# Cosformer attention with a gated MLP on one Trainium2 core: another written order of operations for chunks 3 to 6, with raw loads that wait for each other

## The chip, the cores and the metric

The kernel runs on one core of a Trainium2 chip. The metric is device time in microseconds (us), from start to end of the program on that core; the profile of one such execution shows what each engine did. The engines are TensorE (PE, with its weight loads PEld), VectorE (DVE), ScalarE (ACT), GpSimd (POOL) and SyncE (SP), which here only issues DMAs.

## What is computed

The inputs are q, k and v of shape 8 x 8 x 576 x 64 (batch, heads, positions, head size), and the MLP's `w_in` (512 x 2048), `w_out` (2048 x 512) and `beta` (2048). All are float32, and so is the output of 4608 x 512.

```python
def phi(x, c, s):
    r = np.maximum(x, 0.0)
    return np.concatenate([r * c, r * s], axis=-1)
kv = np.einsum('bhsf,bhsd->bhfd', phi(k), v)
z = np.sum(phi(k), axis=2)
num = np.einsum('bhsf,bhfd->bhsd', phi(q), kv)
den = np.einsum('bhsf,bhf->bhs', phi(q), z)[..., None] + 1e-06
x = (num / den), heads side by side        # 4608 x 512
h = x @ w_in
g = h * (1.0 / (1.0 + np.exp(-beta * h)))
out = g @ w_out
```

Here c and s are cosine and sine of an angle that grows with the position. The attention is linear: per batch and head a 64 x 65 state is summed over all positions, and the numerators and the denominator are products with it.

## The kernel before

**Tiles and chunks.** The MLP runs over 9 chunks of 512 tokens (c = 0 to 8); the attention runs over 8 batches (b = 0 to 7) of 576 tokens, and is laid into the chunks. Chunks 0 to 2 have orders of their own. Chunks 3 to 6 run through one list of names, `ORDER` (L835), chunks 7 and 8 through `ORDER_END` (L842), which has no attention. In chunk c the attention works at batch b = c + 1, prepares keys and values of batch b + 1 and queries of batch b + 2. The order of the list is the order in which `chunk` (L876) issues, and each engine works through its own part of it in that order. Nothing else schedules: waits between engines follow from the data and the buffers.

**A chunk's h phase** makes h and its silu. Four pairs of columns X, Y, Z and V are made by a fast scheme of seven half-size products each (`h_fast`, L456: X1 to X7, and so on); eight further blocks of 128 columns are plain products of four matmuls (p0 to p7, L419), each followed by a silu on ScalarE (sp0 to sp7). Of a pair, `c1` and `cu` are copies on ScalarE, `c5`, `a2`, `a3` and `a7` a copy and three additions on VectorE (`a7` reads the bank that product 4 goes on to write), and `Sa` and `Sb` the two silus. Each chunk uses sums of halves of x as well (t1 to t4, L850), made near the end of the chunk before. `K` is the state of batch b (72 matmuls, L272), `kt` its copy out of PSUM, and sXY (L397) are sums of silu results on VectorE.

**The o phase** begins at `N0`, the numerators of batch b: 144 small matmuls of 65 columns (L293), with a weight load each, in three thirds into PSUM banks 0, 6 and 4. Then come fourteen products of eight matmuls (`o_fast`, L525): ox1 to ox7 and oy1 to oy7, with their copies (c1o, c5o, cuo, c4x, and the same for y) on ScalarE and additions (o2x, o3x, o7x, and for y) on VectorE. Products x5 and y5 share a PSUM bank, and so do x2 and y2. Beside them stand x0, x1 and x2 (denominators, reciprocals and division, three VectorE operations each, and then a DMA transpose into the layout of the MLP, `x_part`, L767); v0 to v8 on ScalarE and w0 to w8 on VectorE, which scale v of batch b + 1 by sine and cosine (L217, L219); k0 to k3, relus of keys on ScalarE; q0 and q1, relus of queries on VectorE (`q_relu`, L196); and g0 and g1, products of turned queries with a tangent on GpSimd (`q_tan`, L255), of which g0 waits for the last sum s that the list has ahead of it.

**Loads and turns.** `load_raw` (L76) issues a DMA of 1,152 KB on SyncE's queue. There is one raw buffer each for q, k and v. `prep` (L857) issues the next load of a kind when the last name of a set has been taken: for k when k0 to k3 and x0 to x2 have been issued, for v after all of v and w, and for queries, after q0, q1 and x0 to x2, first the query turn (`q_turn_dma`, L251, a DMA transpose of the relued queries) and then the load. SyncE issues in this order, and a wait of one DMA holds back those behind it. Output rows are stored by GpSimd's queue up to chunk 6.

```python
        take = prep(b, [
            ({"k0", "k1", "k2", "k3"} | xs_all, lambda: raw_next("k")),
            ({"q0", "q1"} | xs_all, q_next),
            ({f"{o}{n}" for o in "vw" for n in range(NQ)}, lambda: raw_next("v"))])
```

`H_COLS` and `O_COLS` (L848) say which plain products and o products have their matmuls, except the first, issued in two halves of the columns.

Of the kernel before, what the change touches and what calls it, by code (L numbers as in the profile page):

```python
# [22 lines left out]
def kernel(  # L23
# [14 lines left out]
    nc = tc.nc  # L38
# [15 lines left out]
    one = ctx.enter_context(tc.tile_pool(name="one", bufs=1))  # L54
# [12 lines left out]


    raws = {}

    def raw_tile(b, name):
        if (name, b) not in raws:
            raws[name, b] = raw_pool.tile([P, 4, NQ, D], FP32, name=f"raw_{name}", tag=f"raw_{name}")
        return raws[name, b]

    def load_raw(b, name, j0=0, j1=4):  # L76
        js = slice(j0, j1)
        src = {"q": q, "k": k, "v": v}[name][b]
        nc.sync.dma_start(
            out=raw_tile(b, name)[:, js].rearrange("q j n d -> q j (n d)"),  # L80
            in_=src.rearrange("(j g) (p n) d -> (g p) j (n d)", g=2, n=NQ)[:, js, :])

    win = [const.tile([P, MI, 512], BF16, name=f"win{i}") for i in range(4)]
    wout = const.tile([P, JT, DM], BF16, name="wout")
# [41 lines left out]
    GJ = [(0, 0), (0, 1), (1, 0), (1, 1)]  # L126

    load_raw(0, "q", 0, 2)
    load_raw(0, "q", 2, 4)
    beta16 = const.tile([JT, P], FP32, name="beta16")  # L130
    nc.scalar.dma_start(out=beta16, in_=moe_beta.rearrange("(j p) -> j p", p=P))
    load_raw(0, "v", 0, 2)
    load_raw(0, "k", 0, 2)
    load_raw(0, "v", 2, 4)
# [164 lines left out]
    def x_rden(bank, slot, n0, n1, jps):  # L299

        w, m = len(jps), n1 - n0
        nv = ps[:, bank : bank + 2, slot * E : (slot + w * m) * E].rearrange("q j (i s e) -> q j i s e", s=w, e=E)
        den = small.tile([P, 2, m, w], FP32, name="den", tag=f"den{m}{w}")
        nc.vector.tensor_tensor(  # L304
            den, nv[:, :, :, :, D],
            eps9[:, n0:n1].unsqueeze(1).unsqueeze(3).to_broadcast([P, 2, m, w]), op=ALU.add)
        rden = small.tile([P, 2, m, w], FP32, name="rden", tag=f"rden{m}{w}")
        nc.vector.reciprocal(rden, den)
        return nv, rden, n0, jps
# [100 lines left out]
    def h_group(c, jt):  # L410
        h_mm(c, jt)
        h_act(c, jt)
# [95 lines left out]
    def o_mm(c, tt, jts, cols=1):  # L508
        o_ps = ps[:, (2, 3, 0, 1)[tt] if c == 0 else 2 + tt % 2]
        for jt in jts:  # L510
            w = DM // cols if jt > 0 else DM
            for m0 in range(0, DM, w):
                nc.tensor.matmul(o_ps[:, m0 : m0 + w], lhsT=gs[c, jt // 4][:, jt % 4, tt * P : (tt + 1) * P],  # L513
                                 rhs=wout[:, jt, m0 : m0 + w],
                                 start=(jt == 0), stop=(jt == JT - 1 and m0 == DM - w))
        if jts[-1] < JT - 1:
            return
        o_sb = osb_pool.tile([P, DM], FP32, name="o_sb", tag="o_sb")
        nc.scalar.copy(o_sb, o_ps)
        store(c, tt, o_sb)  # L520

    def o_part(c, tt, part, cols=1):
        o_mm(c, tt, range(4 * part, 4 * part + 4), cols)
# [123 lines left out]
    got = x_rden(2, 0, 0, 7, (0,))  # L647
# [17 lines left out]
    got = x_rden(0, 0, 0, 7, (1,))  # L665
# [125 lines left out]
    def one_unit(slot):  # L791
        if slot == 0:
            num_rest()
            att_q(2)
            v_half(2, 0)
        elif slot == 4:
            k_all(2)
        elif slot == 6:
            v_half(2, 1)
        elif slot == 7:  # L800
            q_tan(2, 0)
            q_tan(2, 1)
        elif slot == 12:
            kv_all(2)
        elif slot == 13:
            w_sums(0, 4)
        elif slot == 14:
            att_q(3)
            w_sums(4, 8)
        elif slot == 18:  # L810
            for t, bank in enumerate((4, 6, 0)):
                num_all(2, t, bank)
            for t, bank in enumerate((4, 6, 0)):
                x_part(2, t, bank)
            load_raw(4, "q")
            q_tan(3, 0)
            q_tan(3, 1)
        elif slot == 28:
            v_half(3, 0)

    for slot in range(32):
        if slot < 16:
            h_group(1, slot)
        else:
            o_part(1, (slot - 16) // 4, slot % 4, 2 if slot > 21 else 1)
        one_unit(slot)

    def k_piece(b, j):
# [4 lines left out]
            load_raw(b + 1, "k")  # L833

    ORDER = (  # L835
        "Y1 p1 c1Y X1 p0 X5 c1X c5X X2 X6 K sp0 cuX Y6 X3 a2X kt a3X cuY sp1 X7 SaX a7X p2 Y5 X4 c5Y sp2 "
        "Y2 Z1 a2Y Y7 Y3 c1Z p3 SbX a3Y a7Y SaY Z6 V1 Y4 s01 s03 cuZ Z5 Z2 sp3 Z7 s02 c5Z c1V a7Z s04 "
        "a2Z p4 SbY Z3 sp4 Z4 V5 V6 V2 SbZ a3Z c5V cuV p5 s11 SaZ a2V V3 a3V sp5 s12 V7 s21 SaV p6 a7V "
        "sp6 p7 s22 s13 V4 sp7 s23 s14 SbV s24 s31 s33 N0 ox1 s32 c1o s34 ox5 c5o x0 x1 ox6 ox3 w0 cuo "
        "v3 oy1 v2 v6 ox2 x2 v4 c1y ox7 oy6 cuy o3x o7x oy5 v1 oy7 ox4 k1 g0 g1 c5y w3 q0 o2x t1 w6 t3 "  # L840
        "w1 w2 o7y t2 oy3 v0 c4x v5 v8 w4 q1 oy2 o2y o3y t4 v7 k2 k3 k0 w5 oy4 c4y w8 w7")
    ORDER_END = (  # L842
        "X1 Y5 Y1 X5 c5X p0 c1X X3 c1Y X6 cuX X2 Y6 sp0 c5Y cuY a2X p1 X7 a3X a7X p2 SaX Y7 X4 sp1 Y3 "
        "sp2 a7Y Z1 Y2 Y4 a3Y p3 c1Z Z6 V1 SbX s03 Z5 SbY a2Y Z2 V5 cuZ c1V p4 c5Z a2Z Z7 SaY Z3 V6 c5V "
        "s01 a3Z sp3 sp4 cuV V2 SaZ a7Z V3 a3V p5 a2V p6 sp5 SaV V7 sp6 Z4 p7 s02 a7V s11 SbZ V4 s12 s14 "
        "sp7 SbV oy1 ox1 s21 s13 s31 c1y ox2 s22 s32 ox5 c1o ox6 cuo c5o o2x s34 s24 s33 s04 oy2 s23 oy6 "
        "ox3 o3x cuy ox7 oy5 c5y t3 oy7 t1 o2y o7y oy3 o7x t2 oy4 c4y t4 ox4 o3y c4x")
    H_COLS, O_COLS = {3: 1, 4: 5, 5: 2, 6: 4}, {3: ("45", "25734"), 5: ("4", "25734")}  # L848

    def x_sum(c, kind):  # L850
        xt, n = xt_tile(c), NB // 2
# [107 lines left out]
    for c in range(2, NTC):  # L959
        b = c + 1  # L960
# [77 lines left out]
```

## Time and profile before

| what | value |
|---|---|
| median of three runs | 287.22 us (287.01 to 287.71) |
| the profiled execution | 287.27 us |
| its span | 285.5 us |
| TensorE busy | 272.7 us (96%) |
| VectorE busy | 219.8 us (77%) |
| ScalarE busy | 177.7 us (62%) |
| GpSimd busy | 71.3 us (25%) |
| DMA moved | 54.00 MB, mean 189 GB/s |

The span runs from the first to the last instruction; the execution's own time has some 1.8 us around it. A matmul's end is modelled in this profile, so TensorE's rate is read from starts: a product of four matmuls of 512 columns takes 0.86 us from its first start to the next product's, and one of eight matmuls of 256 columns 0.87 us. "idle before" names what an engine waited for; "issue" there means that nothing in the profile explains the wait. A line number is one of the kernel before.

### The profile page before, as it was taken

Reading aid. Unit: us, or ns where it says so; the run is one execution under the profiler, and the core shown is the slowest. Engines: PE = TensorE matmul, PEld = TensorE weight load, DVE = VectorE, ACT = ScalarE, POOL = GpSimd, SP = SyncE. Lnnn points to the kernel's source line nnn. Section 1 sums busy time; section 2 is a strip of 40 time slices with the busy share of each in tenths; the row PEclk is TensorE's granted clock in tenths of the full one; section 3 lists DMA queues with packets and bytes.
Section 4 is the critical chain, followed back from the end, with each engine's and each line's share of the span. In section 5 each row is a group of like instructions: output and inputs, shape, how many; then the busy total and the mean of one; then the engine's idle time right before and its main releaser. Section 6 shows DMA issues by size and latency. Waiting matters only on the chain. (4 is left out here: it accounts for less than half of the span.)

```text
span 285.5 us, 8867 instructions
## 1 busy us (share of the span) xinstructions
PE 272.7 (96%) x3685; PEld 197.2 (69%) x3685; DVE 219.8 (77%) x547; ACT 177.7 (62%) x356; POOL 71.3 (25%) x89
## 2 busy tenths in 40 slices
PE   8799999999999999999997999999999999999992
PEld 7354455455765688778884787688878866886781
DVE  5989967759999996899879876898689457656840
ACT  5778755863146576965786367955794269329710
POOL 1444000634490182015600632053300220000000
PEclk9999999999999999999999799999999999999998
DMA  6999999999989959973797339817400540032014
GB/s 248 378 393 386 391 380 314 318 247 386 164 251 373 268 103 249 192 282 79 154 285 299 57 77 213 304 30 95 113 2 11 113 110 1 2 85 65 0 39 110
DMA packets 50584, 54.00 MB, mean 189 GB/s; under 512 B 31200, under 2 KB 31472, under 8 KB 50544
## 3 DMA queue, kind: packets, MB, share of 16 engines
q1 hardware_dynamic: 47584, 45.82, 56.1%
q0 software_dynamic: 2688, 7.34, 10.2%
q8 instruction: 29, 0.48, 0.7%
q10 hardware_dynamic: 272, 0.27, 0.3%
q14 instruction: 11, 0.09, 0.2%
HBM read 36.71 MB, written 9.44 MB: 162 GB/s over the span
## 5 line engine op out<-in xcount | busy, mean ns | idle before, releaser
L417 ACT ACTIVATE g_t<-ps,beta 128x512 bf16<-128x512 f32 x96 | 61.3, 693 | 3.5 <-PE ps L426 3.1
L536 PEld LDWEIGHTS <-S 128*128 128x128 bf16 x497 | 45.3, 99 | 6.8 <-issue 1.7
L506 POOL DMA_DIRECT2D out_dram<-o_sb x56 | 31.8, 574 | 71.2 <-DVE o_sb L586 33.8
L426 PE MATMUL ps<-xt,win 128*128 128x512 bf16 (+1 forms) x228 | 48.4, 345 | 0.0
L378 PE MATMUL ps<-xt,win 128*128 128x512 bf16 (+1 forms) x196 | 42.8, 375 | 0.1
L386 ACT ACTIVATE g_t<-ps,beta 128x512 bf16<-128x512 f32 x48 | 32.6, 689 | 10.5 <-PE ps L378 9.9
L536 PEld LDWEIGHTS <-g_t 128*128 128x128 bf16 x378 | 33.5, 99 | 3.8
L378 PEld LDWEIGHTS <-win 128*128 128x128 bf16 x196 | 18.8, 98 | 21.0 <-issue 0.2
L426 PEld LDWEIGHTS <-win 128*128 128x128 bf16 x228 | 22.3, 98 | 12.8
L222 POOL TENSOR_TENSOR qs<-qt,tanr 128x1152 bf16<-128x1152 bf16 x8 | 19.4, 2444 | 45.0 <-DVE den L304 30.1
L219 DVE TENSOR_SCALAR vb<-raw_v,cos 128x256 bf16<-128x256 f32 x63 | 29.6, 518 | 0.3 <-DMA raw_v<-in_v_dram 0.3
L536 PE MATMUL ps<-T,S 128*128 128x256 bf16 (+1 forms) x245 | 28.3, 268 | 1.4 <-DVE o_sb L587 1.4
L513 PE MATMUL ps<-wout,g_t 128*128 128x512 bf16 (+1 forms) x166 | 29.2, 330 | 0.0
L536 PE MATMUL ps<-wout,g_t 128*128 128x256 bf16 (+1 forms) x238 | 28.6, 271 | 0.0
L536 PE MATMUL ps<-wout,S 128*128 128x256 bf16 (+1 forms) x252 | 28.1, 261 | 0.0
L465 PE MATMUL ps<-w_stage 128*128 128x256 bf16 x144 | 26.9, 273 | 0.0
L465 PEld LDWEIGHTS <-w_stage 128*128 128x128 bf16 x192 | 18.4, 98 | 7.4
L315 DVE TENSOR_TENSOR xs<-ps,rden 128x768 bf16<-128x768 f32 (+4 forms) x26 | 22.8, 883 | 0.8
L513 PEld LDWEIGHTS <-g_t 128*128 128x128 bf16 x166 | 15.8, 98 | 10.3
L397 DVE TENSOR_TENSOR S<-g_t 128x512 bf16<-128x512 bf16 (+1 forms) x58 | 22.1, 408 | 0.7 <-ACT g_t L417 0.4
L217 ACT ACTIVATE vb<-raw_v,sin 128x256 bf16<-128x256 f32 (+1 forms) x50 | 21.7, 498 | 1.0 <-DMA raw_v<-in_v_dram 1.0
L490 DVE COPY p<-ps 128x256 f32<-128x256 f32 x24 | 9.9, 421 | 10.8 <-PE ps L465 9.5
(104 smaller groups left out, 402.2 us busy)
## 6 DMA issues: line engine op xcount, KB each, us to landing
raw_v<-in_v_dram SPq DMA_DIRECT2D x7, 1152.0 KB, 11.2
raw_k<-in_k_dram SPq DMA_DIRECT2D x7, 1152.0 KB, 10.0
raw_q<-in_q_dram SPq DMA_DIRECT2D x7, 1152.0 KB, 7.8
out_dram<-o_sb POOLq DMA_DIRECT2D x56, 128.0 KB, 4.3
w_stage<-in_moe_w_in_dram SPq DMA_DIRECT2D x3, 1024.0 KB, 13.7
w_stage<-in_moe_w_out_dram SPq DMA_DIRECT2D x2, 1024.0 KB, 8.5
w_stage<-in_moe_w_out_dram SPq DMA_DIRECT2D x4, 512.0 KB, 11.9
out_dram<-o_sb SPq DMA_DIRECT2D x13, 128.0 KB, 2.4
```

The lines of the kernel that those rows point to most:

```text
L217: nc.scalar.activation(o, a, AF.Copy, scale=t[:, n : n + 1])
L219: nc.vector.tensor_scalar(o, a, scalar1=t[:, n : n + 1], scalar2=None, op0=ALU.mult)
L315: nc.vector.tensor_tensor(o.rearrange("q j n s d -> q j (n s) d"), nv[:, :, a:z, :, 0:D].rearrange("q j n s d -> q j (n s) d"), rden[:, :, ...
L378: nc.tensor.matmul(ps[:, h_bank(c, jt), blocks.start * 64 : blocks.stop * 64], lhsT=win[jt // 4][:, mi, (jt % 4) * P : (jt % 4 + 1) * P], ...
L386: nc.scalar.activation(gs[c, jt // 4][:, jt % 4], ps[:, h_bank(c, jt)], AF.Silu, scale=beta[:, jt : jt + 1])
L397: return nc.vector.tensor_tensor(o, l, r, op=op)
L417: nc.scalar.activation(gs[c, jt // 4][:, jt % 4], ps[:, bank], AF.Silu, scale=beta[:, jt : jt + 1])
L426: nc.tensor.matmul(ps[:, bank, o * 64 : z * 64], lhsT=win[jt // 4][:, mi, (jt % 4) * P : (jt % 4 + 1) * P], rhs=xt[:, o:z, jp, g * HP : (g ...
L465: nc.tensor.matmul(dst, lhsT=left[:, g], rhs=right[:, :, g * HP : (g + 1) * HP], start=start and g == 0, stop=stop and g == 1, skip_group_ ...
L506: eng.dma_start(out=out_v[bb, n][:, m0:m1], in_=o_sb[hf * HP : (hf + 1) * HP, m0:m1])
L513: nc.tensor.matmul(o_ps[:, m0 : m0 + w], lhsT=gs[c, jt // 4][:, jt % 4, tt * P : (tt + 1) * P], rhs=wout[:, jt, m0 : m0 + w], start=(jt == ...
L536: nc.tensor.matmul(dst[:, m : m + w], lhsT=left(i), rhs=right[:, i, m : m + w], start=start and i == 0, stop=stop and i == order[-1], skip ...
```

## The change

Three things are edited. First, every load of a batch above 4 gets a wait on the load issued before it: SyncE doesn't issue it until that one has landed. Second, chunks 3 to 6 get another order. In it the relus of queries q0 and q1 stand in the h phase, ahead of a7Z and a3Z; since they are then done when x2 comes, the query turn is issued directly behind x2's turn and the load of k. p7 and the silus of pair V stand ahead of sp7, GpSimd's g0 and g1 behind the last sum, and most of v and w behind x1 and x2. Third, other products are issued in halves of columns: in chunk 1 from slot 20 on instead of 22, and as `H_COLS` and `O_COLS` say.

```diff
+    last_load = []
     def load_raw(b, name, j0=0, j1=4):
-        nc.sync.dma_start(
+        got = nc.sync.dma_start(
+        if last_load and b > 4:
+            tc.add_manual_dep(got.ins, last_load[-1].ins.name,
+                              mybir.DependencyInfo(mybir.DependencyClass.Sync, mybir.DependencyReason.DATA),
+                              reason="one batch load at a time")
+        last_load.append(got)
...
-            o_part(1, (slot - 16) // 4, slot % 4, 2 if slot > 21 else 1)
+            o_part(1, (slot - 16) // 4, slot % 4, 2 if slot > 19 else 1)
...
     ORDER = (
-        "Y1 p1 c1Y X1 p0 X5 c1X c5X X2 X6 K sp0 cuX Y6 X3 a2X kt a3X cuY sp1 X7 SaX a7X p2 Y5 X4 c5Y sp2 "
-        "Y2 Z1 a2Y Y7 Y3 c1Z p3 SbX a3Y a7Y SaY Z6 V1 Y4 s01 s03 cuZ Z5 Z2 sp3 Z7 s02 c5Z c1V a7Z s04 "
-        "a2Z p4 SbY Z3 sp4 Z4 V5 V6 V2 SbZ a3Z c5V cuV p5 s11 SaZ a2V V3 a3V sp5 s12 V7 s21 SaV p6 a7V "
-        "sp6 p7 s22 s13 V4 sp7 s23 s14 SbV s24 s31 s33 N0 ox1 s32 c1o s34 ox5 c5o x0 x1 ox6 ox3 w0 cuo "
-        "v3 oy1 v2 v6 ox2 x2 v4 c1y ox7 oy6 cuy o3x o7x oy5 v1 oy7 ox4 k1 g0 g1 c5y w3 q0 o2x t1 w6 t3 "
-        "w1 w2 o7y t2 oy3 v0 c4x v5 v8 w4 q1 oy2 o2y o3y t4 v7 k2 k3 k0 w5 oy4 c4y w8 w7")
+        "Y1 c1Y X5 X1 c5X c1X p0 X6 Y6 cuX X2 cuY X3 a2X a3X sp0 K X7 p1 kt Z1 Y5 a7X c5Y X4 SaX sp1 SbX "
+        "Y7 a7Y s01 p2 Y2 s03 Z5 a2Y c1Z sp2 Y4 Y3 SbY Z6 Z2 a3Y SaY p4 V5 a2Z c5Z cuZ s02 c5V V1 p3 q0 "
+        "sp4 Z7 V3 c1V V2 V6 a7Z Z3 sp3 Z4 cuV q1 p5 a3Z a2V SbZ V7 SaZ s11 s04 a3V a7V p6 sp5 s12 p7 "
+        "sp6 s13 SaV V4 s21 s23 s14 SbV s22 N0 sp7 ox1 s31 ox5 s32 k1 x0 c1o s33 ox6 k0 k2 k3 c5o oy1 "
+        "s24 ox2 s34 g0 g1 v8 w4 v4 x1 c1y o2x ox3 v2 v7 cuo x2 oy6 ox7 oy2 cuy o3x o7x oy5 oy7 ox4 w8 "
+        "o2y v6 c5y t1 t3 oy3 w1 w0 o7y t2 v5 v3 oy4 t4 o3y w7 v1 w6 c4x w5 w3 w2 v0 c4y")
...
-    H_COLS, O_COLS = {3: 1, 4: 5, 5: 2, 6: 4}, {3: ("45", "25734"), 5: ("4", "25734")}
+    H_COLS, O_COLS = {4: 5, 6: 5}, {3: ("4", "25734"), 4: ("4", ""), 5: ("4", "25734")}
```

## The prediction

> **What bounds the kernel now.** I read the page's shares first: TensorE is busy for 96% of the span, so only its gaps, its clock and its own work can move the end.
>
> ```profile
> PE 272.7 (96%) x3685; PEld 197.2 (69%) x3685; DVE 219.8 (77%) x547; ACT 177.7 (62%) x356; POOL 71.3 (25%) x89
> ...
> PEclk9999999999999999999999799999999999999998
> ```
>
> One slice of the clock row shows a 7, near 160 us. Next I cut the timeline by chunk at each chunk's first product (110.10, 139.39, 171.43, 200.72, 229.20 us): chunks 3 to 6 take 29.29, 32.04, 29.29 and 28.48 us. Gaps between starts of matmuls give what is lost in each. In all four, 0.37 us in the middle of the numerators (L293), which wait for the last silu of pair V to free PSUM bank 4. In chunks 3 and 5, 0.83 and 0.85 us ahead of product oy5, which waits for addition o3x:
>
> ```profile
> 129.79 2.54 DVE L219 TENSOR_SCALAR vb<-raw_v,cos 128x256 bf16<-128x256 f32 x1
> ...
> 133.58 0.41 DVE L587 TENSOR_TENSOR o_sb<-ps,u 128x256 f32<-128x256 f32 x1
> ```
>
> ```profile
> 127.45 4.73 POOL L222 TENSOR_TENSOR qs<-qt,tanr 128x1152 bf16<-128x1152 bf16 x2 [15.18 <-DVE den L304]
> ```
>
> ```profile
> 134.04 0.55 PE L536 MATMUL ps<-T,S 128*128 128x256 bf16 x6 [0.67 <-DVE o_sb L587]
> ```
>
> A scaling that elsewhere takes 0.35 us (w3, 134.24) takes 2.54 us here, and ends as GpSimd's second tangent product does; x2 and o3x stand behind it on VectorE.
>
> Chunk 4 loses most, by windows of 1 us (columns: window, then busy us of each engine, clock, DMA share, GB/s):
>
> ```profile
> 155.00:156.00 1.00, 0.45 (x32) 0.33 (x31) 1.00 (x3) 0.00 (x0) 0.00 (x0) 1.00 0.31 111
> 156.00:157.00 1.00, 0.00 (x0) 0.00 (x0) 0.90 (x5) 0.00 (x0) 0.23 (x1) 1.00 0.08 25
> 157.00:158.00 1.00, 0.72 (x19) 0.56 (x20) 0.96 (x3) 0.00 (x0) 1.00 (x1) 0.77 0.00 0
> 158.00:159.00 1.00, 1.00 (x6) 0.69 (x5) 0.96 (x2) 0.00 (x0) 1.00 (x1) 0.50 0.06 16
> ```
>
> TensorE stops for 2.0 us inside the numerators, and the clock is then 0.50 for 3.4 us (16 products at 213 ns instead of 109: 1.66 us). No engine is named as releaser ("issue"). The DMA queues show what it is:
>
> ```profile
> q8 instruction: 29, 0.48, 0.7%
> ```
>
> 29 blocks of 16 KB are TensorE's some 7,370 instructions[...]. The stall falls at instruction 4,526; the block was fetched only at 154.71 to 155.74, while raw loads filled the DMA (share about 1.0 from 145 to 155), and its predecessor was used up in 1.5 us, as it lay wholly in the numerators (288 instructions).
>
> [...]
>
> **The change, part by part.** Chunk c works with batch b = c+1; q0 and q1 are the relus of batch b+2, so they exist in chunks 3 and 4 only.
>
> *New order of the o phase (gain).* I walked it with the trace's spacings: 0.34 us per addition or sum on VectorE, 1.33 per x part, 0.87 per o product, 0.25 from a product's end to its reader. Numerators start at +14.3 us in the chunk. The last four sums end at +19.2, and only then GpSimd starts; w4 is issued ahead of it; x1, o2x, x2 and o3x read PSUM, and such operations ran beside GpSimd at 127.6 to 129.8. So o3x ends at 19.4+1.3+0.3+1.3+0.4 = +22.8, and oy5, now one product later, begins at +23.8. That stall (0.83, 0.85) goes, with 1 us to spare. Silu SbV moves ahead of sp7; the chain sp6, SaV, SbV still ends at +15.3 against +15.2 needed: 0.2 of the 0.37 stays. o3y no longer comes after oy4: 0.14 saved behind chunk 6. A chunk without waits is 28.48-0.37-0.14 = 27.97 us; with 0.2 and 0.1 for split products, 28.25.
>
> *Columns.* 7 halves more in chunk 1, 3 fewer in chunk 3's p0, 7 moved from chunk 3 to 4, 6 fewer, 3 more: a pair of halves costs 2 to 5 ns more than the whole, under 0.05 us in sum. They move block boundaries: counted in the built order, the numerators of chunks 3 to 6 start 64 after one, 1 after, 78 after and 5 ahead before the change, and 72 after, 5 ahead, 74 after and 3 ahead now. Chunk 4 still has a whole block inside, as chunk 6 has without a stall, where the DMA is idle.
>
> *Relus of queries in the h phase (loss).* The wait is not new, its place is. q0 now stands on VectorE ahead of a7Z, and Z4 on TensorE needs a7Z. Unhindered, q0 would start at +9.5 us and Z4 at +11.1. The h phase otherwise has room: VectorE's 16 additions and copies, kv, 11 sums and two relus are 16x0.34+0.6+11x0.34+2x0.67 = 11.1 us before the numerators at 14.3. What decides is when the raw queries land. For chunk 3 these are batch 6, loaded in chunk 2, which isn't changed:
>
> ```profile
> 105.70 0.92 SPq L79 DMA_DIRECT2D raw_k<-in_k_dram  x1
> 106.79 8.14 SPq L252 DMA_TRANSPOSE qt<-qb  x1
> 115.06 0.50 SPq L79 DMA_DIRECT2D raw_q<-in_q_dram  x1
> ```
>
> ```profile
> raw_q<-in_q_dram SPq DMA_DIRECT2D x1, 1152.0 KB, 10.3
> raw_v<-in_v_dram SPq DMA_DIRECT2D x1, 1152.0 KB, 12.6
> ...
> qt<-qb SPq DMA_TRANSPOSE x1, 14.5
> ```
>
> The turn lands at 121.3, the queries at 115.06+10.3 = 125.4. Before, q0 ran at 134.50. In the trace's packets the load starts at 119.5, when the turn's end, and a load moves in 3 to 3.9 us. Without v's load behind it (now one at a time) it should land at about 124.0 (loads alone land 0.9 us after their last packet: 83.5, 100.7). X5, which moves up to +0.22, waits 0.25 us for the sum of x that chunk 2 ends at 110.51. So Z4, due at 110.1+0.25+11.1 = 121.45, comes at 124.0+0.1+0.67+0.43+0.05 = 125.25: 3.8 us idle (3.0 to 4.1). Such a gap must halve the clock: a gap of 2.0 cost 1.66, so I take 1.6 (0.8 to 2.5). Chunk 3: 28.25+0.25+5.4 = 33.9, +4.6 us.
>
> *Query turn behind x2, loads one at a time.* In chunk 3 SyncE issues k's load at +24.7 (x2's turn, +23.4, takes 1.25), 3.6 us before chunk 4, then the turn; the queries' load (batch 7) waits for k's landing, then runs behind the turn's packets. Unhindered that is k 3, turn 3.2 (140.1 to 143.3), the eight output stores between (1 MB, 4 to 5), q 3.2: landing at +10.5 to +13 of chunk 4. The same sequence took 17.8 us from k's issue at 105.70, which would be +14.2. Before +9.8 nothing waits. I take +12.3: Z4 comes 12.3+1.25-11.1 = 2.5 us late (0 to 4.4), with 1.0 for a clock that drops in part of the cases. v's load then issues at about +12.5 and lands before its readers at +19 (delayed by the same wait). Behind the wait, the block for chunk 4's numerators is asked for before v's packets run: the 2.0 us of fetch and 1.66 of clock go; up to 1.5 if not. Chunk 4: 28.25+3.5 = 31.75, -0.3. In chunk 5 v's load lands about +12, before use. GpSimd's tangents wait for nothing new, its stores go out about 1 us earlier.
>
> *Sum:* +4.6-0.3-1.0 (chunk 5) -0.3 (chunk 6) = +3.0. Chunks 7 and 8 keep their list. The profiled execution took 287.27 us for a span of 285.5, the median is 287.22: the base is the same, 287.3+3.0 = **290.3 us**.
>
> **Rivals.** *Late in both chunks by the longer chain.* Chunk 4 then takes 28.25+4.4+1.7 and 1.5 for the fetch, +3.8: 287.3+4.6+3.8-1.3 = 294.4. For it: k to q took 17.8 us when stores ran beside. *Late in chunk 3 only.* Batch 7 lands by +10: chunk 4 gives 3.1 to 3.8; total 286.7 to 287.5, no change. For it: the two other turns landed 8.8 and 8.9 us after issue, not 14.5. *Faster: the queries are there.* If both loads land before +9.8, every gain stands: -1.0-3.8-1.0-0.3 = -6.1, 281.2 us. It decides at 119.9 us in chunk 3; against it stands that the turn's packets only end then, for it only an earlier turn. *That it doesn't do what it says:* the built order shows q0 ahead of a7Z with waits for both DMAs, so no.
>
> **How the numbers follow.** Forecast (late in both, spread 288.2 to 292.5) 0.62; longer chain 0.10; chunk 3 only 0.18; faster 0.10. About 0.3% is what a measurement of this kernel can tell from no change (286.4 to 288.1). Faster 0.11, same 0.17, slower 0.72. The range leaves out the fastest case and the top of the longer chain: 286.6 to 293.0; the forecast's own is 288.2 to 292.5.
>
> **What would show it.** In chunk 3 VectorE idle before L200's relu of queries until about 124, released by the raw q load, TensorE idle 3.8 us before a product of pair Z with DVE as releaser, and a clock dip there; the same, shorter, in chunk 4; no 2.5 us scaling beside GpSimd; no gap before oy5; no "issue" gap of 2 us in the numerators. I am wrong if batch 6 lands before 121, or if the relu's wait doesn't reach Z4.

## The result and the profile after

The changed kernel takes 297.11 us (median of 294.95, 296.48, 297.73, 302.11) where the kernel before takes 287.47 beside it: a ratio of 1.031, interval 1.024 to 1.037, so it is slower. The prediction said slower, but 290.3 us and at most 293.0. Ratios here and below leave disturbed executions out, so they need not be the quotient of the medians.

The profiled execution of the changed kernel is the one of 294.95 us, the fastest of the four, with a span of 293.0. First the page: TensorE's share, its clock, and the chain that ended last.

```profile
PE 275.6 (94%) x3686; PEld 198.4 (68%) x3686; DVE 216.5 (74%) x547; ACT 178.6 (61%) x356; POOL 71.1 (24%) x89
...
PEclk9999999999999999979998699999999999999999
...
PE ps L542 25%; DMA raw_q<-in_q_dram 13%; PE ps L432 12%; PE ps L384 10%; PE ps L471 9%; PE ps L519 7%; DMA w_stage<-in_moe_w_in_dram 4%; PE ps L299 3%; DMA raw_k<-in_k_dram 3%; SPq L258 2%; PE ps L278 2%; DMA xt<-xs 1%; DVE win L121 1%; SPq L80 1%; PE ps L240 0%
```

Two things are new. The clock row has two dips, a 7 and a 6, where it had one. And in the chain, a load of raw queries carries 13% of the span: the end now hangs on a DMA, where before it hung on TensorE's own work.

TensorE's timeline at the two places (start, duration, engine, line, operation; in brackets idle time before it and what ended it):

```profile
121.41 0.38 PE L471 MATMUL ps<-xt,w_stage 128*128 128x256 bf16 x2
125.89 0.58 PE L471 MATMUL ps<-w_stage,win 128*128 128x256 bf16 x2 [4.09 <-DVE ps L499]
...
155.32 0.38 PE L471 MATMUL ps<-xt,w_stage 128*128 128x256 bf16 x2
160.83 0.58 PE L471 MATMUL ps<-w_stage,win 128*128 128x256 bf16 x2 [5.12 <-DVE ps L499]
```

Each pair of lines is Z3 and Z4. From start to start 4.37 and 5.40 us pass where 0.11 would: Z4 waits for addition a7Z (L499) on VectorE. VectorE's timeline tells why a7Z is late:

```profile
124.73 0.76 DVE L200 TENSOR_SCALAR qb<-raw_q 128x1152 bf16<-128x1152 f32 x1 [4.58 <-DMA raw_q<-in_q_dram]
...
159.67 0.76 DVE L200 TENSOR_SCALAR qb<-raw_q 128x1152 bf16<-128x1152 f32 x1 [5.62 <-DMA raw_q<-in_q_dram]
160.35 0.43 DVE L499 TENSOR_TENSOR ps<-ps,p 128x256 f32<-128x256 f32 x1
```

The relu q0 stands idle until the raw queries land, and a7Z runs directly behind it. Behind the second gap the clock is what costs (windows of 1 us: length, busy us of PE, PEld, DVE, ACT and POOL, clock, DMA share, GB/s):

```profile
158.00:159.00 1.00, 0.00 (x0) 0.00 (x0) 0.00 (x0) 0.00 (x0) 0.00 (x0) 1.00 0.65 240
159.00:160.00 1.00, 0.00 (x0) 0.00 (x0) 0.33 (x1) 0.00 (x0) 0.00 (x0) 0.82 0.01 5
...
161.00:162.00 1.00, 1.00 (x4) 0.43 (x3) 1.00 (x3) 0.55 (x1) 0.00 (x0) 0.50 0.65 164
...
165.00:166.00 1.00, 1.00 (x4) 0.39 (x3) 1.00 (x4) 0.71 (x2) 0.00 (x0) 0.50 0.00 0
166.00:167.00 1.00, 1.00 (x13) 0.37 (x15) 0.01 (x1) 0.55 (x1) 0.00 (x0) 0.76 0.00 0
```

At 158 to 159 no engine works at all and the DMA still moves data. Then p5, V7, p6 and p7 run at 0.50. The dip lasts 6.83 us, twice the 3.41 of chunk 3.

What the loads did is on SyncE's timeline:

```profile
105.97 0.85 SPq L80 DMA_DIRECT2D raw_k<-in_k_dram  x1
106.93 8.06 SPq L258 DMA_TRANSPOSE qt<-qb  x1
115.25 0.37 SPq L80 DMA_DIRECT2D raw_q<-in_q_dram  x1
...
141.93 0.58 SPq L80 DMA_DIRECT2D raw_k<-in_k_dram  x1
142.61 6.90 SPq L258 DMA_TRANSPOSE qt<-qb  x1
149.57 0.85 SPq L80 DMA_DIRECT2D raw_q<-in_q_dram  x1
159.65 0.37 SPq L80 DMA_DIRECT2D raw_v<-in_v_dram  x1
```

SyncE is busy with issuing the query turn for 8.06 and 6.90 us, and until then it issues nothing else. The queries' load of batch 7 goes out at 149.57 and lands 10.0 us later. For half of these its bytes don't move. The DMA queues from 149.6 to 154.6 us (packets, MB, share of the 16 engines' time):

```profile
q1 hardware_dynamic: 877, 0.22, 57.6%
q0 software_dynamic: 232, 0.61, 53.9%
```

q1 is SyncE's queue, q0 GpSimd's with the output stores. 0.22 MB in 877 packets are 256 bytes each, the packets of the turn; a raw load comes in packets of 2,304 bytes. So the turn's packets move, beside the stores, until 155.5, and the queries' begin at 154.9.

The wait before oy5 is gone, as walked. VectorE's scaling w4, which stood at 129.79 for 2.54 us before, GpSimd's tangents, and oy5 on TensorE:

```profile
135.31 0.35 DVE L225 TENSOR_SCALAR vb<-raw_v,cos 128x256 bf16<-128x256 f32 x1
...
135.64 4.73 POOL L228 TENSOR_TENSOR qs<-qt,tanr 128x1152 bf16<-128x1152 bf16 x2 [23.11 <-DVE S L403]
...
140.02 1.05 PE L542 MATMUL ps<-T,S 128*128 128x256 bf16 x15
```

The scaling is over as GpSimd starts and takes 0.35 us; the last line, oy5, has no idle time before it. Why it took 2.54 us beside GpSimd before isn't shown.

### The profile page after: what moved, and what is told of

Same layout as the page of the kernel before. It is cut to its first block, busy times and chain, and to the rows that moved or that the text cites. A ratio compares the mean times of both kernels' runs of the same rounds, so it can differ in the third digit from the quotient of the medians.

```text
span 293.0 us, 8873 instructions
## 1 busy us (share of the span) xinstructions
PE 275.6 (94%) x3686; PEld 198.4 (68%) x3686; DVE 216.5 (74%) x547; ACT 178.6 (61%) x356; POOL 71.1 (24%) x89
## 4 chain that ended last, share of the span: by engine, by line
PE 69%; DMA 22%; SPq 3%; DVE 2%; issue 1%; ACTq 0%; ACT 0%; DVEq 0%
PE ps L542 25%; DMA raw_q<-in_q_dram 13%; PE ps L432 12%; PE ps L384 10%; PE ps L471 9%; PE ps L519 7%; DMA w_stage<-in_moe_w_in_dram 4%; PE ps L299 3%; DMA raw_k<-in_k_dram 3%; SPq L258 2%; PE ps L278 2%; DMA xt<-xs 1%; DVE win L121 1%; SPq L80 1%; PE ps L240 0%
## 5 line engine op out<-in xcount | busy, mean ns | idle before, releaser
L432 PE MATMUL ps<-xt,win 128*128 128x512 bf16 (+1 forms) x222 | 51.9, 369 | 0.0
L542 PEld LDWEIGHTS <-S 128*128 128x128 bf16 x490 | 44.6, 98 | 4.6
L384 PE MATMUL ps<-xt,win 128*128 128x512 bf16 (+1 forms) x196 | 42.8, 375 | 0.1
L542 PEld LDWEIGHTS <-g_t 128*128 128x128 bf16 x385 | 33.6, 98 | 3.5
L384 PEld LDWEIGHTS <-win 128*128 128x128 bf16 x196 | 18.8, 98 | 21.1 <-issue 0.4
L432 PEld LDWEIGHTS <-win 128*128 128x128 bf16 x222 | 22.7, 102 | 15.2 <-issue 3.1
L519 PE MATMUL ps<-wout,g_t 128*128 128x256 bf16 (+1 forms) x173 | 29.3, 324 | 0.0
L542 PE MATMUL ps<-wout,g_t 128*128 128x256 bf16 (+1 forms) x238 | 27.8, 266 | 0.0
L225 DVE TENSOR_SCALAR vb<-raw_v,cos 128x256 bf16<-128x256 f32 x63 | 23.5, 431 | 0.1
L471 PEld LDWEIGHTS <-win 128*128 128x128 bf16 x144 | 14.1, 98 | 13.6 <-issue 10.0
L519 PEld LDWEIGHTS <-g_t 128*128 128x128 bf16 x173 | 16.5, 98 | 9.6
```

Of the source, the lines that this page charges most:

```text
L225: nc.vector.tensor_scalar(o, a, scalar1=t[:, n : n + 1], scalar2=None, op0=ALU.mult)
L384: nc.tensor.matmul(ps[:, h_bank(c, jt), blocks.start * 64 : blocks.stop * 64], lhsT=win[jt // 4][:, mi, (jt % 4) * P : (jt % 4 + 1) * P], ...
L432: nc.tensor.matmul(ps[:, bank, o * 64 : z * 64], lhsT=win[jt // 4][:, mi, (jt % 4) * P : (jt % 4 + 1) * P], rhs=xt[:, o:z, jp, g * HP : (g ...
L471: nc.tensor.matmul(dst, lhsT=left[:, g], rhs=right[:, :, g * HP : (g + 1) * HP], start=start and g == 0, stop=stop and g == 1, skip_group_ ...
L542: nc.tensor.matmul(dst[:, m : m + w], lhsT=left(i), rhs=right[:, i, m : m + w], start=start and i == 0, stop=stop and i == order[-1], skip ...
```

## Where the time went, chunk by chunk

Each chunk is cut at its first product, as in the prediction. Of two profiled executions of the changed kernel the first is the one shown, the second is the run after_again.

| us | before | predicted | after | after_again |
|---|---|---|---|---|
| chunk 3 | 29.29 | 33.9 | 34.12 | 35.36 |
| chunk 4 | 32.04 | 31.75 | 36.07 | 36.67 |
| chunk 5 | 29.29 | 28.3 | 28.15 | 28.14 |
| chunk 6 | 28.48 | 28.2 | 28.07 | 28.08 |

From before to after this is +4.83, +4.03, -1.14 and -0.41; with chunk 3's start 0.26 later it makes +7.57, and the profiled times differ by 294.95 - 287.27 = 7.68. In this execution only chunk 4 is off the prediction by more than 0.3 us. In that of after_again, 296.97 us and nearer to the median, chunk 3 is off by 1.5 us as well.

## The experiments

Chunk times below come from one profile of each kernel (that of swap_both is of an execution of 290.26 us, over its median); the medians of the kernel before, run beside them, were 286.8 to 287.6 us.

| kernel | relus of queries | loads wait | SyncE's order | median us | ratio (interval) | chunk 3 | chunk 4 |
|---|---|---|---|---|---|---|---|
| after_again | h phase | yes | k, turn, q | 297.48 | 1.035 (1.028 to 1.041) | 35.36 | 36.67 |
| no_chain | h phase | no | k, turn, q | 298.24 | 1.037 (1.032 to 1.043) | 36.09 | 37.83 |
| turn_first | h phase | no | turn, k, q | 294.62 | 1.023 (1.019 to 1.027) | 37.37 | 34.31 |
| swap_both | h phase | yes | turn, q, k | 287.89 | 0.996 (0.992 to 0.999) | 32.26 | 33.28 |
| swap_no_chain | h phase | no | turn, q, k | 282.34 | 0.983 (0.977 to 0.989) | 28.39 | 29.12 |
| swap_shift | h phase | no | turn, q, k | 281.60 | 0.981 (0.977 to 0.986) | 28.44 | 28.59 |
| q_late | h phase, later | yes | k, turn, q | 288.64 | 1.000 (0.997 to 1.004) | 30.74 | 32.04 |
| q_back | o phase | yes | k, turn, q | 286.18 | 0.997 (0.994 to 0.999) | 33.00 | 30.26 |
| order_alone | o phase | no | k, turn, q | 285.80 | 0.994 (0.991 to 0.997) | 28.63 | 32.51 |
| order_shift | o phase | no | k, turn, q | 282.59 | 0.984 (0.979 to 0.989) | 28.44 | 29.60 |
| chain_alone | as before | yes | as before | 290.03 | 1.005 (1.003 to 1.008) | 30.51 | 33.95 |
| fetch_shift | as before | no | as before | 285.27 | 0.992 (0.989 to 0.994) | 29.34 | 29.22 |

The kernel warm, without a ratio, follows below. In every kernel with the new order, warm apart, chunks 5 and 6 take 28.14 and 28.07 us within 0.02.

**The theory**: the relus hold Z4 until the raw queries land, and they land late because of what stands ahead of their load on SyncE. **The rivals**: another part of the change costs the time (order, columns, waiting loads), or the waiting loads make the queries late.

### The relus moved back

```diff
-V1 p3 q0 sp4 ... Z4 cuV q1 p5 ... t1 t3 oy3 ... o3y w7
+V1 p3 sp4 ... Z4 cuV p5 ... t1 t3 q0 oy3 ... o3y q1 w7
```

> The changed kernel with q0 and q1 moved back into the o phase (behind t3 and o3y), all else kept. Theory (the relus of queries, standing ahead of a7Z, hold Z4 until the raw queries land): the gaps of 4.3 us before Z4 in chunk 3 and 5.3 us in chunk 4 vanish, and with them the half clock behind each (1.5 and 2.8 us); the time is 281 to 285 us, the upper end if the instruction block of chunk 4's numerators is again fetched late. Rival (another part of the change, such as the columns or the serial loads, slows the kernel): it stays at 292 us or more.

Both gaps before Z4 went, and the time fell to 286.18 us, not to 281 to 285. A new wait took their place: in chunk 3's o phase TensorE lost 4.6 us, 2.5 of them in one gap and most of the rest by the half clock behind it (from 135.24 eight matmuls take 1.66 us instead of 0.87). The timelines of this kernel, VectorE, ScalarE and TensorE:

```profile
132.96 1.80 DVE L225 TENSOR_SCALAR vb<-raw_v,cos 128x256 bf16<-128x256 f32 x1 [3.31 <-DMA raw_v<-in_v_dram]
...
132.96 0.92 ACT L223 ACTIVATE vb<-raw_v,sin 128x256 bf16<-128x256 f32 x2 [3.07 <-DMA raw_v<-in_v_dram]
133.78 0.35 ACT L588 COPY p<-ps 128x256 f32<-128x256 f32 x1
...
134.17 1.03 PE L542 MATMUL ps<-T,S 128*128 128x256 bf16 x8 [2.37 <-ACT p L588]
```

The scalings v8 (ScalarE) and w4 (VectorE) wait for v of batch 5, whose load stands behind the queries' landing and so issued at 126.16 instead of near 116. Behind v8 stands the copy c1y, and oy6 on TensorE needs its bank. In the changed kernel this wait is not seen, since the gap before Z4 had put everything 4 us later. So the change has a second late load under the first.

### Without the waits between loads

```diff
-        if last_load and b > 4:
+        if False:
```

> The changed kernel without the wait of each load on the load before it; order and columns kept. Theory (in chunk 4 the query load was held by SyncE, which was busy 6.9 us with the query turn, not by the wait on k's load): k of batch 7 landed at 148.7 us and the query load was issued at 149.57, so both gaps before Z4 stay within 1 us of 4.3 and 5.3 us; the late instruction block of chunk 4's numerators may return (0 to 3.7 us); 292 to 299 us. Rival (the serial loads make the queries late): chunk 4's gap drops to 2 us or less and the time to 289 us or less.

> The changed kernel with q0 and q1 back in the o phase and without the wait between loads: only the new order of the rest and the columns are left. Theory (the new order gains by itself; what remained in the run with the relus moved back alone, 4.6 us in chunk 3 and 2.0 in chunk 4 of the o phase, was the wait of w4 and v8 for v, whose load was held behind the query load): v's load issues near 116 us instead of 126, no gap in the o phase of chunks 3 to 6, no gap before Z4; 280 to 284 us, the upper end if chunk 4's instruction block is fetched late again. Rival (the order itself makes those gaps): they stay, 285 us or more.

In no_chain (the changed kernel without the waits) neither side was right on chunk 4. The gap didn't fall, which the rival wanted, but grew from 5.3 us to 8.0, where I had allowed 1 us. Chunk 3's gap grew too, to 5.6 us. The query load of chunk 4 was issued at about the same place (+5.5 us in the chunk, +5.1 with the waits) but landed at +17.8 instead of +15.1 (+15.6 in after_again). v's load, issued right behind it at 152.24, is not seen to slow it: by the packets, v's follow the queries', and v landed 3.0 us after them. What took longer is the turn, whose packets ran beside the stores for 11.0 us, until 160.1, against 8.3 us in the changed kernel; why is open. So the queries landed 2.2 to 2.7 us earlier with the waits, without a reason shown.

order_alone (q_back without the waits) shows what the rest of the change is worth: chunk 3 takes 28.63, so nearly all of q_back's 4.6 us were v's late load. Chunk 4 lost 4.0 us again, to the gap in the numerators that the kernel before has too (2.64 us) and to the half clock behind it (0.53 from 158 to 161 us). Its 285.80 us is over the 280 to 284 expected, and meets the rival's number, though not its gaps in the o phase: the range had room for that gap only on top of 280, and the best kernel below, without it, takes 281.6. The four medians are 285.8 and 286.2 with the relus in the o phase, without and with waits, and 298.2 and 297.5 with them in the h phase: the place of the relus costs 11 to 12 us, the waits at most 1.

### The same waits alone

> The kernel before with only the wait of each batch load on the load before it. Theory (the 2.0 us stop in chunk 4's numerators is an instruction block fetched late behind raw loads that fill the DMA): with loads one at a time the block comes earlier, the stop shrinks or goes and the half clock with it, 283.5 to 286 us. Rival (the wait itself delays loads that somebody needs): 288 us or more, with a new gap released by a raw load. Third: the stop is of another origin, 287.2 us with the same 2.0 us gap.

The kernel before with only the waits took 290.03 us: slower by 0.5%, as the rival said. The gap in chunk 4's numerators did shrink, from 2.0 to 1.0 us without a dip, but v's readers then waited in both chunks (1.2 us more in chunk 3). The theory was right on the fetch and wrong on the time.

### The block of instructions

```diff
-    H_COLS, O_COLS = {3: 1, 4: 5, 5: 2, 6: 4}, ...
+    H_COLS, O_COLS = {3: 8, 4: 5, 5: 2, 6: 4}, ...
```

> The kernel before with 8 instead of 1 of chunk 3's plain products issued in halves: 28 more matmuls ahead, so that the boundaries of TensorE's instruction blocks move, and chunk 4's numerators start 43 instructions before a boundary rather than 1 after one. Theory (late instruction block): the 2.0 us stop in the middle of chunk 4's numerators and the 1.66 us of half clock go or move to another place; 283.5 to 285 us, or about 287 if the stop only moves. Rival (the stop belongs to the numerators' data or banks): the gap stays at the same matmul and the time is 287.2 us.

The edit adds 21 matmuls, not 28, each with its weight load: 42 instructions. Chunk 4 went from 32.04 to 29.22 us and the stop with it: 285.27 us. The next test moves the same boundaries in order_alone:

```diff
-    H_COLS, O_COLS = {4: 5, 6: 5}, ...
+    H_COLS, O_COLS = {3: 7, 4: 5, 6: 5}, ...
```

> The run with the new order of the rest alone (relus of queries back in the o phase, no wait between loads), and 7 of chunk 3's plain products in halves: 42 more instructions on TensorE ahead of chunk 4, whose numerators then start 37 after a block boundary rather than 5 ahead of one. Theory (the 4.0 us that chunk 4 lost there, numerators and half clock, are the late instruction block): they go, chunk 4 takes 28.5 us instead of 32.5, 281 to 282.5 us. Rival (the new order feeds the numerators late): the gap stays, 285 us or more.

Here 1.3 us of it stayed (chunk 4 29.60, not 28.5), and just this settles what it is. TensorE's timeline in chunk 4's numerators of order_shift, and then of swap_no_chain, which lacks the 42 instructions:

```profile
153.94 0.21 PE L299 MATMUL ps<-kv,qs 64*64 64x65 bf16 x2
155.45 0.22 PE L299 MATMUL ps<-kv,qs 64*64 64x65 bf16 x2 [1.30 <-issue]
```

```profile
154.41 0.21 PE L299 MATMUL ps<-kv,qt 64*64 64x65 bf16 x3
155.45 0.21 PE L299 MATMUL ps<-kv,qt 64*64 64x65 bf16 x1 [0.82 <-issue]
```

In the first the gap stands 42 instructions earlier in the program, in another product of the numerators. But counted from the program's start it is the same one: in the records of the kernel before, order_alone, order_shift, swap_no_chain and q_late alike, the gap is ahead of TensorE's instruction 4,531 (the prediction had 4,526; 2.02, 2.64, 1.49, 1.01 and 2.92 us from start to start), and in chain_alone and swap_both ahead of 4,525, where a few records can be missing. It belongs to a count, not to a product, so it is the block. The packets of the instruction queue agree: in all seven the gap ends 1.3 to 1.5 us after those of one block do. That also explains fetch_shift. There the block's packets ended at 154.0 us, in order_shift at 154.2; but TensorE reached the count at 155.75 in the first and waited for nothing, and stood before it from 153.96 in the second. What decides when the block's packets come isn't shown; that it is "asked for before v's packets run" was an estimate of the prediction. How many instructions a block holds is an estimate: in the kernel before, 29 packets of 16 KB came for TensorE's 7,370 recorded instructions, 254 for each; the boundaries counted in the prediction and in the two expectations above are estimates too.

### The queries' load ahead of k's

```diff
         take = prep(b, [
-            ({"k0", "k1", "k2", "k3"} | xs_all, lambda: raw_next("k")),
             ({"q0", "q1"} | xs_all, q_next),
+            ({"k0", "k1", "k2", "k3"} | xs_all, lambda: raw_next("k")),
...
-            for j in range(4):
-                k_piece(b + 1, j)
             for n in ("a7", "a2", "a3"):
                 x[n]()
             att_q(b + 2)
+            for j in range(4):
+                k_piece(b + 1, j)
```

> The changed kernel with the query turn and the query load issued ahead of the load of k, in chunk 2 and in chunks 3 and on. Theory (what counts is when the queries land, not where their relus stand): batch 6 lands near +9 of chunk 3 and batch 7 before +9 of chunk 4, both gaps before Z4 fall below 1 us and the clock stays full; the time is 281 to 284 us. Rival (relus in the h phase cost by themselves, by VectorE's time ahead of a7Z): gaps of 1 us or more stay though the queries have landed, and the time is 287 us or more.

> The changed kernel with the query turn and load ahead of k's load, and without the wait between loads; the relus of queries stay in the h phase. Theory (queries landed before +9.5 of chunk 3 and near +10 of chunk 4, v no longer held behind k): gap before Z4 below 1 us in chunk 3 and below 2 us in chunk 4, no wait for v in the o phase; 281 to 285 us. Rival (all loads at once share the DMA, so that the queries land no earlier than with the wait, or an instruction block is late): 286 us or more, with the gap where the theory has none.

> The run with query turn and load ahead of k's load, without the wait between loads, and with the same 42 more instructions in chunk 3. Theory (of the 29.1 us of chunk 4 there, 1.0 is the late instruction block, the rest is work): chunk 4 takes 28.2 us and the time is 281 to 282 us. Rival (what is left in chunk 4 is data of the numerators): no change, 282.3 us.

With the waits (swap_both) the gap before Z4 is gone in chunk 3 and is 1.3 us in chunk 4, and the mean clock is 0.997 (0.982 in the changed kernel), but v, now last of three, lands at 132.3 and is waited for: 287.89 us, against 281 to 284 expected, for the theory had overlooked v. Without the waits both gains stand together: 282.34 us, and 281.60 (281.30 to 282.30) with the boundaries moved, 1.9% under the kernel before (interval 1.4 to 2.3). The relus in the h phase cost nothing by themselves: order_shift, which has them in the o phase, took 282.59 us. SyncE and VectorE in swap_shift:

```profile
135.47 4.48 SPq L258 DMA_TRANSPOSE qt<-qb  x1
140.00 0.84 SPq L80 DMA_DIRECT2D raw_q<-in_q_dram  x1
140.94 0.47 SPq L80 DMA_DIRECT2D raw_k<-in_k_dram  x1
...
149.31 0.76 DVE L200 TENSOR_SCALAR qb<-raw_q 128x1152 bf16<-128x1152 f32 x1 [0.84 <-DMA raw_q<-in_q_dram]
```

### The turn ahead of k's load, the queries' load behind it

swap_both and its kin change two things: the turn no longer stands behind k's load, and k's bytes no longer run ahead of the queries'. turn_first changes only the first, in chunk 3 and on; `q_turn` and `q_load` are the two halves of `q_next`.

```diff
         take = prep(b, [
+            ({"q0", "q1"} | xs_all, q_turn),
             ({"k0", "k1", "k2", "k3"} | xs_all, lambda: raw_next("k")),
-            ({"q0", "q1"} | xs_all, q_next),
+            ({"q0", "q1"} | xs_all, q_load),
```

> The changed kernel without the wait between loads, and with the query turn of chunks 3 and on issued ahead of k's load instead of behind it; the query load stays last of the three, and chunk 2 stays as it is. Theory (SyncE spends 7 to 8 us on a turn that stands behind k's load and 3.4 to 4.5 us on one that doesn't, and this holds the query load back): the turn takes at most 4.5 us, the query load issues 3 us sooner and lands at +11.5 to +14 of chunk 4 instead of +17.8; chunk 4's gap before Z4 falls from 8.0 to 1.5 to 4 us, chunk 3 stays; 291 to 294 us where the kernel with k's load ahead takes 298.2. Rival (the bytes of k's load ahead of the queries' cost it, whatever the turn): landing at +16 or later, gap 6 us or more, 296 us or more.

SyncE and VectorE, first of turn_first, then of no_chain, which differs only in this:

```profile
144.42 4.30 SPq L258 DMA_TRANSPOSE qt<-qb  x1
148.81 0.53 SPq L80 DMA_DIRECT2D raw_k<-in_k_dram  x1
149.40 0.72 SPq L80 DMA_DIRECT2D raw_q<-in_q_dram  x1
...
161.02 0.76 DVE L200 TENSOR_SCALAR qb<-raw_q 128x1152 bf16<-128x1152 f32 x1 [4.04 <-DMA raw_q<-in_q_dram]
```

```profile
143.15 1.05 SPq L80 DMA_DIRECT2D raw_k<-in_k_dram  x1
144.31 7.21 SPq L258 DMA_TRANSPOSE qt<-qb  x1
151.57 0.57 SPq L80 DMA_DIRECT2D raw_q<-in_q_dram  x1
...
163.95 0.76 DVE L200 TENSOR_SCALAR qb<-raw_q 128x1152 bf16<-128x1152 f32 x1 [8.31 <-DMA raw_q<-in_q_dram]
```

The turn takes SyncE 4.30 us instead of 7.21, and the queries land at +13.5 of the chunk instead of +17.8. Chunk 3, whose turn is issued in chunk 2 as ever (8.63 us), keeps its gap, at 6.2 us. So of chunk 4's lateness without the waits, 17.8 - 13.5 = 4.3 us go with the turn's place behind k's load. k's bytes ahead are worth 3.2 us against swap_shift (+10.3) and 5.2 against swap_no_chain (+8.3). The theory's reason, that SyncE's time holds the query load back, isn't what the packets show: in no_chain that load was issued at 151.57, but nine tenths of its packets moved only after the turn's had ended, at 160.1. Ahead of k's load the turn's packets were through at 149.8, before most of the stores; behind it they ran beside them for 11.0 us. The time, 294.62 us, lies 0.6 above the range of the theory, since chunk 3 was longer.

### The clock behind the gap, and the relus a little later

```diff
+                if op == "Z4" and c in (3, 4):
+                    for _ in range(36):
+                        nc.tensor.matmul(ps[:, 2, 256:512], lhsT=win[0][:, 0, 0:P], rhs=win[0][:, 1, 0:256], ...)
```

> The changed kernel with 36 products of no use (128 x 256 each, about 109 ns, into a free half of a PSUM bank) ahead of Z4 in chunks 3 and 4: 3.9 us of work where TensorE waits 4.3 to 6 us; outputs stay those of the reference. Theory (behind each gap the half clock costs a further 1.5 to 2.9 us): the clock stays at 1.0 in chunk 3 and mostly in chunk 4, Z4 comes as late as before, and 2.5 to 4.5 us go: 292.5 to 295 us where the changed kernel beside it takes 297.4. Rival (the clock is no separate cost, or the products delay Z4 more than they save): 297 us or more.

TensorE in chunk 3, and the windows behind the gap in both chunks:

```profile
121.23 4.09 PE L939 MATMUL ps<-win 128*128 128x256 bf16 x36
126.33 0.38 PE L471 MATMUL ps<-w_stage,win 128*128 128x256 bf16 x2 [1.01 <-DVE ps L499]
```

```profile
127.00:128.00 1.00, 1.00 (x7) 0.57 (x6) 1.00 (x4) 1.00 (x3) 0.00 (x0) 1.00 0.95 343
...
161.00:162.00 1.00, 1.00 (x7) 0.53 (x6) 1.00 (x5) 1.00 (x3) 0.00 (x0) 1.00 1.01 382
```

Z4 comes as late as ever (chunk 3: 5.1 us behind Z3), but the clock stays at 1.00. Chunks 3 and 4 take 33.49 and 33.65 us, 1.9 and 3.0 less than in after_again, whose relus start at like places (+15.0 and +15.7 against +15.2 and +15.5 here). Chunk 5 lost 1.1 us of this at another gap of "issue", ahead of instruction 5,553, that is 1,022 behind 4,531, or about four blocks at the estimated 254. The four times were 292.32, 292.50, 297.18 and 299.75; they lie too far apart for a ratio, so the saving stands on the profiles alone.

> The changed kernel with q0 and q1 later in the h phase, behind a7V, the last addition of pair V, so that Z4 and V4 no longer stand behind them (loads and turn as in the changed kernel). Theory (what counts is the place of the relu against the landing at +14 to +16 us): the gaps before Z4 go; VectorE waits some 1 to 3 us for the queries before the last sums, which ox5 and later products need; the v loads, held behind the query loads, come late for w4 and v8 by up to 4 us: 284 to 291 us. Rival (the stall moves on undiminished to the next product that needs VectorE): 294 us or more.

With both relus behind a7V (`a3V a7V q0 q1 p6`) the gaps before Z4 went; q0 still waited 1.8 and 3.4 us (4.58 and 5.62 in the changed kernel), and 2.4 us were lost from ox5 to oy1 in chunk 3, for VectorE was late with the sums and x0. 288.64 us, as the theory expected: the later the place of the relus, the less the same landing cost here.

### The changed kernel once more

> The changed kernel itself once more, for a second profile and for the spread of its times (294.95 to 302.11 us so far). Theory (the extra time over the profiled execution is a later landing of the same raw queries): where the execution is longer than 295 us, the gaps before Z4 in chunks 3 and 4 are longer by the difference, with the half clock behind them, and nothing else moves by over 0.5 us. Rival (another place): the two gaps keep 4.3 and 5.3 us, and the difference lies in the o phases or in chunks 0 to 2.

The second profile's span is 2.1 us longer: the gaps are 4.98 and 5.93 us from start to start instead of 4.37 and 5.40, and the half clock in chunk 3 covered more of the work. Chunks 3 and 4 hold 1.84 of the 2.1 us. So an execution of 297 us differs from the one of 294.95 by a later landing of the same queries, at +14.9 and +15.6 us of their chunks instead of +14.3 and +15.1; why the landing varies so is open.

## Why the prediction was wrong

**Right.** The path: q0's wait for the raw queries, a7Z behind it, Z4 behind that. In chunk 3 of the profiled execution the size was near too: the landing was +14.3 us against the +13.9 that 124.0 us means, the gap 4.26 us beyond its normal spacing against 3.8 (just outside the stated 3.0 to 4.1), the half clock 1.5 against 1.6. But that is the fastest execution. In after_again the landing was +14.9, the gap 4.87 and the half clock lasted 6.83 us, so chunk 3 took 35.36 us where 33.9 was forecast. The wait before oy5 went (chunk 5: -1.14 against -1.0). Of the 0.37 us in the numerators I kept 0.2; about 0.1 is left (1.43 us for the numerators in chunks 3, 5 and 6 against 1.36 in chunk 4). The late block of chunk 4 didn't strike in either profile of the changed kernel, as forecast. And had the queries been there in time, I gave 281.2 us; swap_no_chain took 282.34 us and swap_shift 281.60.

**The step that failed** is the landing in chunk 4: "Unhindered that is k 3, turn 3.2 (140.1 to 143.3), the eight output stores between (1 MB, 4 to 5), q 3.2 ... I take +12.3". It was +15.1. Of the 2.8 us, 1.05 is where the sequence begins: k's load went out 2.55 us before chunk 4 instead of 3.6, for a turn of x ahead took 2.20 us on SyncE instead of 1.2. The other 1.75 is the sequence: 17.65 us from k's issue to the landing, where +12.3 allowed 15.9 and the four terms make 13.4 to 14.4. By the packets, k's load needed 6.4 us from its issue to its last packet (148.3), where the sum has 3: its first packet came after 1.5 us, and they moved for 4.8. The turn and the stores beside it took 7.2 us more (155.5), and their terms make 7.2 to 8.2. The queries needed 4.1 us more to the landing, where the sum has 3.2. So the loads were sized too small, each as the time for which its bytes move at best, without its start, its landing and what runs beside it. The trace before showed the whole: the sequence that began with k's load at 105.70 had taken 17.8 us by the prediction's own reading. I had that number in front of me and gave it to a rival at 0.10. It gave 294.4 us; the profiled execution took 294.95 and the median is 297.11. That the rival comes so near is partly luck: it counted 1.5 us for a late block, which didn't come, and too little for the wait and the clock (4.4 and 1.7 against 5.3 and 2.8).

**The second step** followed from it: "with 1.0 for a clock that drops in part of the cases". Behind 5.3 us the clock dropped in both profiles and for twice as long: 2.8 us. Chunk 4 thus: gap 5.3 instead of 2.5, clock 2.8 instead of 1.0, and 0.3 less elsewhere, +4.3 on 31.75.

**What the rivals got wrong.** That the waits between loads make the queries late fell with no_chain, where the queries came later still. That order or columns cost time fell with order_alone and order_shift.

## What to carry to other kernels

A step that waits for a load can be moved earlier only after the load has been: find the landing, not the issue, and subtract. When a sequence of DMAs on one queue already ran once in the trace, its whole length (here 17.8 us from k to q) is a better estimate than a sum of terms picked from elsewhere: it then took 17.65 us where the terms made 13.4 to 14.4, and one of them, the query turn, took SyncE from 3.08 to 8.63 us in these runs. And expect the next wait behind the one you remove: here it was v's load, hidden by the first, which cost chunk 3 of q_back 4.6 us.

## What the runs showed of the hardware

**The query turn took SyncE longest close behind a plain load.** The 576-token query turn took SyncE 6.5 to 8.6 us to issue within 1.5 us behind a load of 1,152 KB (in no_chain 7.85 and 7.21, in turn_first's chunk 2 8.63), 5.6 to 6.3 us when it came some 4 us after such a load (order_alone 6.14 and 6.27), 4.9 us when it came 5 us after (order_shift), and 3.3 to 3.6 us when it came 9 us after (near 70 us in every kernel). With a turn of x directly ahead of it instead, it took 3.1 to 5.6 us (before 3.08, swap_no_chain 5.16 and 3.37, turn_first 4.30). Why wasn't measured. A load issued behind the turn isn't late for this alone: in the changed kernel's chunk 4 its bytes began to move only 5.3 us after its issue, as the turn's ended.

**The clock didn't follow the gap's length alone.** From chunk 3 on, over all profiles, gaps up to 1.9 us between starts of products left the clock at 1.00. Of six from 2.0 to 3.0 us, four halved it (2.02, 2.64, 2.65, 3.02) and two did not (2.16 and 2.92, in chain_alone and q_late). All eight from 3.8 us up halved it, seven of them for 6.83 us; the eighth (4.37), and every shorter gap that did, for 3.41. In the clock records of the changed kernel the stretches at 1.00 between these changes last 116.05, 30.72 and 126.29 us, 34, 9 and 37 times 3.413 us; in those of the kernel before 150.19 and 122.88, 44 and 36 times. Why a gap of 2.02 us halved the clock and one of 2.92 didn't isn't shown.

**A late instruction block cost 0.8 to 2.7 us,** and its place went by the count of instructions: the same 4,531 in five kernels, with 42 instructions added ahead or without. Such a stop stands in eight of the fifteen profiles. In all eight TensorE went on 1.3 to 1.5 us after the block's packets had ended. The DMA wasn't full at each of them: ahead of the gap in warm (193.13 to 194.34 us), in chunk 5's o phase, the DMA share was 0.00 to 0.07.
